# Attention followed by a mixture of experts on one core: expert blocks chosen from step 1 on, two to four steps ahead, with GpSimd padding the last ones

## The chip, the core and the metric

The kernel runs on one core of one Trainium2 chip. The metric is the device time of one execution in microseconds (us); less is better. Beside it stands a profile of one execution: its span is the time from the first to the last instruction.

## What is computed

Four batches of 5056 tokens go through a channel attention (256 x 256 per batch), and each of the 20224 resulting tokens goes through one of eight experts.

```python
# attention, for each batch; q, k, v are (4, 5056, 256)
qn = q / (norm(q, axis=1) + 1e-6);  kn = k / (norm(k, axis=1) + 1e-6)
a = softmax(kn.T @ qn / tau)                      # 256 x 256
x = (v @ a).reshape(20224, 256)

# routing: one expert of eight per token
logits = x @ w_gate + modality_bias[modality_id]
e_idx = argmax(logits, axis=1);  gate_w = softmax(logits)[e_idx]

# experts: w1 is (8, 256, 1024), w2 is (8, 1024, 256)
for e in range(8):
    mask = e_idx == e
    out[mask] = gate_w[mask, None] * (relu(x[mask] @ w1[e]) @ w2[e])
```

With the inputs used, the routing is uneven: 10112 tokens go to expert 7, 8704 to expert 4, 1408 to expert 6 and none to the others.

## The kernel before

**Steps.** The tokens are taken in 40 steps of 512 (ten for each batch; the tenth of a batch has 448). Step g does these things:

- `va_pieces`: it loads a tile of v (two buffers), transposes it (`vtp`), multiplies it by the batch's attention matrix (`xp`, 24 matmuls a step) into token rows `x`, and routes them (`route`): per-expert counts by small matmuls (`rp`), a place `pi` for each token, and four indirect DMAs on GpSimd that scatter the rows to `xs` in HBM, where each expert has a stretch of its own. The running end of each expert's rows is `bases[g]`. The load and the transposes of step g+1 stand in step g.
- `kq_pieces`: for the next batch (so in steps 0 to 29) it loads a tile of q and of k, splits each into a high and a low part, and adds their product to the 256 x 256 matrix `g`. The first batch's q and k work stands before step 0.
- at the first step of a batch, `softmax_pieces` makes the attention matrix.

**Blocks.** The experts work on blocks of 512 rows of one expert (40 blocks; the last two have 384 rows). At the end of a step, `pick` chooses a block on VectorE: among the experts that have at least 512 rows not yet taken, the one with the lowest number. It writes the first row and the expert's number to `pki`. If no expert has 512 rows, it takes spare rows behind all experts, which are filled with zeros and an out-of-range token number. `slots_by(g)` says how many blocks are chosen by step g; `START` sets the first. A chosen block goes to the list `waiting` and is begun `LAG` steps later.

`block_pieces` makes a block's pieces: `load_w` (register loads of `pki` on SyncE, then two halves of `w1` and `w2` into `w1r` and `w2r`, three buffers each), `load_x` (the block's rows from `xs` into `xr`, after all scatters of the steps up to the choice and after the pads), `split_w` (weights into high and low parts, ScalarE and VectorE), `tr_x` (transposes `xtp`), `m1` (`hp`, relu into `hh` and `hl`), `m2` (`y`) and `finish` (scaled rows `yo`, scattered to the output by GpSimd). The weights and rows of a block are loaded at the start of the step before it begins; its `split_w` and `tr_x` are put into the second half of the body of the block before it. For the first block they stand at the end of the step before.

**Order.** `_interleave` merges the pieces of a step's block, its attention work and its q and k work in proportion. The program's scheduler then fixes the order of the instructions of each engine when the program is built; an engine runs them in that order and waits where something is missing. SyncE issues all loads, GpSimd all scatters.

**Buffers in the first steps.** As long as no block runs, q and k of the second batch borrow the blocks' buffers: loads use `w1r` and `w2r` for `2 <= s < START + 2`, splits use `xh` and `xl`, squares `hh` and `hl` for `s < START + 1`. Steps before `first_block = LAG + START` use the blocks' PSUM buffers for transposes and routing.

**The end.** After step 39, SyncE writes a block of pad rows behind the last row of each expert (eight DMAs of 516 KB, each at a row number read by a register load). Then the remaining blocks run; the last three ("tail" blocks, slots 37 to 39) are chosen among all rows that are left, full blocks first. Behind them stands a conditional part for rows still left, which is not entered with these inputs.

Of the kernel before, what the change touches and what calls it, by code (L numbers as in the profile page):

```python
# [34 lines left out]
def kernel(  # L35
# [35 lines left out]
    LAG = 4  # L71
# [10 lines left out]
    const = ctx.enter_context(tc.tile_pool(name="const", bufs=1))  # L82
    p1 = ctx.enter_context(tc.tile_pool(name="p1", bufs=1))
# [45 lines left out]
    eid9 = const.tile([1, E + 1], F32, name="eid9")  # L129
    nc.vector.memset(eid9, 0.0)  # L130
    nc.vector.tensor_copy(eid9[:, 0:E], iof[0:1, :])
    prio9 = const.tile([1, E + 1], F32, name="prio9")
    nc.vector.memset(prio9, 0.5)
    nc.vector.tensor_copy(prio9[:, 0:E], desc[0:1, :])
    inc9 = const.tile([1, E + 1], F32, name="inc9")
    nc.vector.memset(inc9, 0.0)
    nc.vector.memset(inc9[:, 0:E], float(BLK))
    nxt9 = const.tile([1, E + 1], F32, name="nxt9")
    nc.vector.memset(nxt9, float(E * CAP))
    nc.vector.tensor_copy(nxt9[:, 0:E], base0[0:1, :])  # L140
    end9 = const.tile([1, E + 1], F32, name="end9")
    nc.vector.memset(end9, float(E * CAP + BLK))

    xs = dram.tile([ROWS, XW], F32, name="xs")
    pad = {}
# [6 lines left out]
    pads = []  # L152
    written = [[] for _ in range(G)]

    def pad_rows(r):
        ins = nc.sync.dma_start(
            xs[bass.ds(r, BLK), :].rearrange("(p t) c -> p t c", t=BLK // P),
            pad[0].unsqueeze(1).to_broadcast([P, BLK // P, XW]),
        )
        pads.append(ins.ins)  # L160
        tc.declare_no_dep(
            ins.ins, group="xr", reason="pads go past the last row of an expert, and before the blocks with them"
        )

    small = {}
# [274 lines left out]
    first_block = LAG + START  # L440

# [122 lines left out]
    def tiles(slot):  # L564
        return TT - 1 if NB_MIN - SHORT <= slot < NB_MIN else TT

    def pick(g, slot, tail):
        nc.vector.tensor_copy(end9[:, 0:E], bases[g][0:1, :])
        sh = [1, E + 1]
        rem = p2.tile(sh, F32, tag="rem", name=f"rem_{slot}")  # L570
        nc.vector.tensor_tensor(rem, end9, nxt9, ALU.subtract)
        pr = p2.tile([1, 2, E + 1], F32, tag="pr", name=f"pr_{slot}")
        if tail:

            full = pr[:, 1, 0:E]
# [6 lines left out]
        m = p2.tile([1, 1], F32, tag="pm", name=f"pm_{slot}")  # L582
# [4 lines left out]
        pk = p2.tile([1, 2], F32, tag="pk", name=f"pk_{slot}")  # L587
        nc.vector.tensor_reduce(pk, pr, AX.X, ALU.add)
        pki = p4.tile([1, 2], I32, tag="pki", name=f"pki_{slot}")
        nc.vector.tensor_copy(pki, pk)  # L590
        nc.vector.scalar_tensor_tensor(rem, rem, tiles(slot) / TT, inc9, ALU.mult, ALU.mult)
        nc.vector.tensor_tensor(nxt9, nxt9, rem, ALU.add)
        return pki

    FH = FF // 2
    JH = NJ // 2
    FCH = 2 * P

    def block_pieces(g, slot, pki, tail):
        st = {"wr": {}, "wc": {}, "h": {}}  # L600
        tt = tiles(slot)
        rows = tt * P
# [1 line left out]
        def load_x():  # L604
            r = nc.sync.value_load(pki[0:1, 0:1], min_val=0, max_val=E * CAP)
            xr = p3.tile([P, TT, XW], F32R, tag="xr", name=f"xr_{slot}")
            ins = nc.sync.dma_start(
                xr[:, 0:tt, :].bitcast(F32), xs[bass.ds(r, rows), :].rearrange("(p t) c -> p t c", t=tt)
            )
# [140 lines left out]
    for s in range(NS):  # L750
        run(kq_pieces(0, s))
        if s == 0:
            load_small()
            make_pad("pad0")
            pad_rows(E * CAP)
    setup_bias(0)
    run(softmax_pieces(0))
    setup_bias(1)
# [12 lines left out]
    def block_stream(blk, nxt):  # L771

        once(blk, "load")
        once(blk, "prep")
        body = list(blk["body"])
        if nxt is not None:
            once(nxt, "load")
            done.add((nxt["slot"], "prep"))
            at = [len(body) * (i + 4) // 8 for i in range(len(nxt["prep"]))]
            for o, f in reversed(list(zip(at, nxt["prep"]))):  # L780
                body.insert(o, f)
        before = open_blk[0]["last"] if open_blk[0] is not None else []
        open_blk[0] = blk
        return [blk["first"]] + before + body
# [3 lines left out]
    for g in range(G):  # L788
        b, s = divmod(g, NS)
        streams = []  # L790
        for gg, blk in waiting:
            if gg <= g - LAG + 1:
                once(blk, "load")
        if len(waiting) > 0 and waiting[0][0] <= g - LAG:
            _, blk = waiting.pop(0)
            streams.append(block_stream(blk, waiting[0][1] if waiting and waiting[0][0] <= g - LAG + 1 else None))
# [5 lines left out]
        if waiting and waiting[0][0] <= g - LAG + 1:  # L802
# [44 lines left out]
    def left_over(slot, n):  # L847
        if n <= 0:
            return
        rem = p1.tile([1, E + 1], F32, tag="lrem", name=f"lrem_{slot}")  # L850
        nc.vector.tensor_tensor(rem, end9, nxt9, ALU.subtract)
# [44 lines left out]
```

## Time and profile before

| | |
|---|---|
| median of 3 runs | 1243.62 us (1242.7 to 1243.8) |
| the profiled execution | 1244.48 us, span 1242.2 us |
| mean granted TensorE clock | 0.996 |
| TensorE (PE) busy | 1222.2 us, 98% |
| its weight loads (PEld) | 1115.3 us, 90% |
| VectorE (DVE) busy | 843.0 us, 68% |
| ScalarE (ACT) busy | 755.0 us, 61% |
| GpSimd (POOL) busy | 347.9 us, 28% |
| HBM read and written | 167.06 MB and 46.34 MB |

How the rows below are read: the page cuts the span into 40 equal slices and gives for each the busy share in tenths, and the granted clock (PEclk) likewise. A row of a timeline has the start and the duration in us, engine, line, operation and tiles, and in square brackets the idle time before it and what ended it. A row of waits says who waited for whom: us in total, times, longest. A row of DMA issues has the issuing queue, how many, their size, and the median us from issue to landing. SPq is SyncE's queue of DMA issues. `L523` is line 523 of the kernel.

### The profile page before, as it was taken

To read this page: it belongs to the slowest core of one execution; us is meant where nothing else is said; L and a number is where in the kernel's file an instruction comes from. 1 tells how busy PE (TensorE), PEld (TensorE's weight loads), DVE (VectorE), ACT (ScalarE), POOL (GpSimd) and SP (SyncE) were. 2 spreads that over 40 slices of the span, in tenths; PEclk is the share of its full clock that TensorE was granted. 3 is DMA by queue.
4 is the path that set the end of the run, shared out by engine and by line. 5 is a ranking of instruction groups with operands and counts; after the bars stand their busy time and mean duration, and the time that the engine had idled before them with its cause. 6 is when DMAs were issued, how large, how long until landed. Compare 5 with 4: busy or idle time off the path is not lost.

```text
span 1242.2 us, 23800 instructions
## 1 busy us (share of the span) xinstructions
PE 1222.2 (98%) x8316; PEld 1115.3 (90%) x8316; DVE 843.0 (68%) x2215; ACT 755.0 (61%) x1531; POOL 347.9 (28%) x348
## 2 busy tenths in 40 slices
PE   7998999999999999999999999999999999999997
PEld 6897999999999999999999999999999999999997
DVE  7997967767777667867677776666655666665552
ACT  7885856766666666766666665565555555545553
POOL 0135243232222222322222222222432222321121
PEclk9998999999999999999999999999999999999999
DMA  9769864565555555555555554444554443467320
GB/s 321 245 207 302 262 197 155 160 194 176 173 178 173 171 171 171 168 171 170 174 185 183 171 166 136 136 135 147 162 178 153 143 153 121 147 208 222 119 95 29
DMA packets 113026, 215.06 MB, mean 173 GB/s; under 512 B 16128, under 2 KB 61696, under 8 KB 112896
## 3 DMA queue, kind: packets, MB, share of 16 engines
q1 hardware_dynamic: 97632, 171.84, 44.2%
q0 software_dynamic: 15264, 41.60, 8.8%
q8 instruction: 67, 1.10, 0.4%
q14 instruction: 63, 0.52, 0.1%
HBM read 167.06 MB, written 46.34 MB: 172 GB/s over the span
## 4 chain that ended last, share of the span: by engine, by line
PE 89%; issue 3%; DVE 3%; DMA 2%; ACT 1%; POOL 1%; SPq 0%; POOLq 0%; DVEq 0%; ACTq 0%
PE hp L677 34%; PE y L697 34%; PE xp L487 9%; PE g L283 4%; PE vtp L471 2%; PE g L287 2%; PE xtp L659 2%; DMA k<-in_k_dram 1%; POOL out_dram L418 1%; PE selfk L294 0%; DVE acc L274 0%; DMA xs<-x,pi 0%; DVE ks L258 0%; DMA xr<-xs 0%; DMA q<-in_q_dram 0%
## 5 line engine op out<-in xcount | busy, mean ns | idle before, releaser
L697 PE MATMUL y<-w2h,hh 128*128 128x256 f32 x1264 | 356.8, 282 | 0.6 <-ACT yo L713 0.6
L418 POOL DMA_INDIRECT xs<-x,pi x160 | 171.9, 1074 | 660.9 <-ACT w1h L645 480.3
L697 PE MATMUL y<-w2l,hh 128*128 128x256 f32 x1264 | 352.9, 279 | 0.0
L697 PE MATMUL y<-w2h,hl 128*128 128x256 f32 x1264 | 351.8, 278 | 0.1
L683 DVE SCALAR_TENSOR_TENSOR hl<-hp,hh 128x512 fp32r<-128x512 f32 (+1 forms) x320 | 216.5, 677 | 145.8 <-ACT hh L682 145.5
L682 ACT ACTIVATE hh<-hp 128x512 fp32r<-128x512 f32 (+1 forms) x320 | 190.2, 594 | 170.4 <-PE hp L677 168.5
L677 PE MATMUL hp<-xh,w1h 128*128 128x512 f32 (+1 forms) x640 | 256.7, 401 | 0.2 <-ACT xh L664 0.2
L677 PE MATMUL hp<-xl,w1h 128*128 128x512 f32 (+1 forms) x640 | 251.3, 393 | 0.0
L677 PE MATMUL hp<-xh,w1l 128*128 128x512 f32 (+1 forms) x640 | 250.7, 392 | 0.0
L697 PEld LDWEIGHTS y<-w2h,hh 128*128 128x128 f32 x1264 | 237.5, 188 | 12.6 <-ACT yo L713 0.8
L697 PEld LDWEIGHTS y<-w2l,hh 128*128 128x128 f32 x1264 | 238.1, 188 | 10.0
L697 PEld LDWEIGHTS y<-w2h,hl 128*128 128x128 f32 x1264 | 236.7, 187 | 0.4 <-DVE hl L683 0.3
L418 POOL DMA_INDIRECT out_dram<-yo,xr x158 | 162.5, 1029 | 157.5 <-ACT yo L713 113.9
L649 DVE TENSOR_TENSOR w2l<-w2r,w2h 128x512 fp32r<-128x512 f32 x160 | 110.3, 690 | 71.8 <-ACT w2h L645 71.7
L645 ACT CAST w2h<-w2r 128x512 fp32r<-128x512 f32 x160 | 100.0, 625 | 77.4 <-PE y L697 68.4
L649 DVE TENSOR_TENSOR w1l<-w1r,w1h 128x512 fp32r<-128x512 f32 x160 | 109.8, 687 | 52.1 <-ACT w1h L645 51.8
L677 PEld LDWEIGHTS hp<-xh,w1l 128*128 128x128 f32 x640 | 120.7, 189 | 26.3
L645 ACT CAST w1h<-w1r 128x512 fp32r<-128x512 f32 x160 | 100.9, 631 | 55.6 <-PE hp L677 55.2
L677 PEld LDWEIGHTS hp<-xl,w1h 128*128 128x128 f32 x640 | 121.0, 189 | 14.0 <-DVE xl L665 0.2
L677 PEld LDWEIGHTS hp<-xh,w1h 128*128 128x128 f32 x640 | 120.6, 189 | 13.6 <-ACT xh L664 0.3
L283 PE MATMUL g<-qs,ks 128*128 128x512 f32 (+1 forms) x320 | 120.5, 400 | 6.7 <-DVE qs L258 5.5
L487 PE MATMUL xp<-ah,vh 128*128 128x264 f32 x320 | 96.1, 301 | 0.1
(152 smaller groups left out, 1829.6 us busy)
## 6 DMA issues: line engine op xcount, KB each, us to landing
w1r<-in_moe_w_dram SPq DMA_DIRECT2D x80, 512.0 KB, 3.4
w2r<-in_moe_w_dram SPq DMA_DIRECT2D x80, 512.0 KB, 3.7
xr<-xs SPq DMA_DIRECT2D x38, 516.0 KB, 4.8
v<-in_v_dram SPq DMA_DIRECT2D x36, 512.0 KB, 5.3
q<-in_q_dram SPq DMA_DIRECT2D x35, 512.0 KB, 8.1
k<-in_k_dram SPq DMA_DIRECT2D x35, 512.0 KB, 5.7
xs<-pad SPq DMA_DIRECT2D x9, 516.0 KB, 6.0
xs<-x,pi POOLq DMA_INDIRECT x160, 5.0
```

What stands on the lines that cost most here:

```text
L283: nc.tensor.matmul(g, ks[:pp, t, m * P : (m + 1) * P], qs[:pp, t, :], start=first, stop=False, skip_group_check=True,)
L287: nc.tensor.matmul(g[:, 0:C], ks[:pp, t, C + m * P : C + (m + 1) * P], qs[:pp, t, 0:C], start=False, stop=last, skip_group_check=True,)
L418: ins = nc.gpsimd.indirect_dma_start(out=dst, out_offset=bass.IndirectOffsetOnAxis(ap=idx, axis=0), in_=rows, in_offset=None, bounds_check ...
L471: nc.tensor.matmul(tp[:, t * P : (t + 1) * P], st["v"][:, t, h * P : (h + 1) * P], ident, is_transpose=True, start=t == 0, stop=True, skip ...
L487: nc.tensor.matmul(xp[:, 0:DE], a[:, h, t * P : (t + 1) * P], w[:, h, :], start=i == 0, stop=i == len(seq) - 1,)
L645: ins = nc.scalar.copy(hi, src).ins
L649: nc.vector.tensor_tensor(lo, src, hi.bitcast(F32), ALU.subtract)
L659: nc.tensor.matmul(tp[:, t * P : (t + 1) * P], st["xr"][:, t, h * P : (h + 1) * P], identr, is_transpose=True, start=t == 0, stop=True, sk ...
L677: nc.tensor.matmul(hp[:, 0:rows], w[:, h, fs], x[:, h, 0:rows], start=i == 0, stop=i == len(seq) - 1)
L682: nc.scalar.activation(hh[:, 0:rows], hp[:, 0:rows], AF.Relu)
L683: nc.vector.scalar_tensor_tensor(hl[:, 0:rows], hp[:, 0:rows], 0.0, hh[:, 0:rows].bitcast(F32), ALU.max, ALU.subtract)
L697: ins = nc.tensor.matmul(y, a[:, tsl], w[:, j % 2, :], start=(j == 0 and i == 0 and t % 2 == 0), stop=(j == NJ - 1 and i == 2), skip_group ...
```

## The change

The first block is chosen in step 1 instead of 3, and no block is chosen in steps 7 and 13. A block is begun four steps after its choice up to the one chosen in step 6, three steps after for those of steps 8 to 12, and two steps after from step 14 on, so that one block begins in each step from 5 to 39. The pads behind the experts' ends are gone, apart from the spare rows. Instead `pick` runs on 128 partitions, and for a tail block it works out, for each of the block's rows past the expert's last, its place in `xs`; GpSimd scatters pad rows there (four or three indirect DMAs per tail block; rows that hold tokens get a number out of range, and nothing is written for them). The block's `load_x` waits for those scatters.

```diff
-    START = 3
+    START = 1
+
+    SKIP = (7, 13)
...
+    rowid = {TT: eid[:, E + 1 : E + 1 + TT], TT - 1: eid[:, E + 1 + TT : E + 2 * TT]}
+    for tt in rowid:
+        nc.gpsimd.iota(io_i[:, 0:tt], pattern=[[1, tt]], base=0, channel_multiplier=tt)
+        nc.vector.tensor_copy(rowid[tt], io_i[:, 0:tt])
...
     def slots_by(g):
-        return max(0, g + 1 - START)
+        return max(0, g + 1 - START - sum(x <= g for x in SKIP))
+
+    def lag(g):
+        n = LAG
+        for x in SKIP:
+            n -= g >= x + n
+        return n
...
     def pick(g, slot, tail):
...
+        if not tail:
+            return pki, pads
+        tt = tiles(slot)
+        row = room[:, 4 * (E + 1) : 4 * (E + 1) + tt]
+        nc.vector.tensor_scalar(row, rowid[tt], pk[:, 2:3], float(BADTOK), ALU.is_lt, ALU.mult)
+        at = pki[:, 2 : 2 + tt]
+        nc.vector.scalar_tensor_tensor(at, rowid[tt], pk[:, 0:1], row, ALU.add, ALU.add)
+        return pki, [
+            scatter(
+                xs[:, :], at[:, t : t + 1], pad[0], ["x", "xr"] + [f"x{i}" for i in range(G)], [], ROWS - 1,
+                "past the last row of an expert, and before the block with them",
+            )
+            for t in range(tt)
+        ]
...
-            after(ins.ins, pads if tail else pads[:1])
+            after(ins.ins, padded)
...
-            if gg <= g - LAG + 1:
+            if gg <= g + 1 - lag(g + 1):
                 once(blk, "load")
-        if len(waiting) > 0 and waiting[0][0] <= g - LAG:
+        if len(waiting) > 0 and waiting[0][0] <= g - lag(g):
...
-    endi = p1.tile([1, E], I32, tag="endi", name="endi")
-    nc.vector.tensor_copy(endi, bases[G - 1][0:1, :])
+    p1.tile([P, 8], F32, tag="filler", name="filler")
     make_pad("pad1")
-    for e in range(E):
-        r = nc.sync.value_load(endi[0:1, e : e + 1], min_val=0, max_val=E * CAP)
-        pad_rows(r)
```

More of the change, by code (lines that the diff above doesn't have):

```diff
@@ L127 @@
     nc.vector.tensor_scalar(base0, iof, float(CAP), None, ALU.mult)
[L129 to L132, printed above, removed]
+    eid = const.tile([P, 16], F32, name="eid9")
+    nc.vector.memset(eid, 0.0)
+    eid9 = eid[:, 0 : E + 1]
+    nc.vector.tensor_copy(eid9[:, 0:E], iof)
+    prio9 = const.tile([P, E + 1], F32, name="prio9")
     nc.vector.memset(prio9, 0.5)
-    nc.vector.tensor_copy(prio9[:, 0:E], desc[0:1, :])
-    inc9 = const.tile([1, E + 1], F32, name="inc9")
+    nc.vector.tensor_copy(prio9[:, 0:E], desc)
+    inc9 = const.tile([P, E + 1], F32, name="inc9")
     nc.vector.memset(inc9, 0.0)
     nc.vector.memset(inc9[:, 0:E], float(BLK))
-    nxt9 = const.tile([1, E + 1], F32, name="nxt9")
+    nxt9 = const.tile([P, E + 1], F32, name="nxt9")
     nc.vector.memset(nxt9, float(E * CAP))
-    nc.vector.tensor_copy(nxt9[:, 0:E], base0[0:1, :])
-    end9 = const.tile([1, E + 1], F32, name="end9")
+    nc.vector.tensor_copy(nxt9[:, 0:E], base0)
+    end9 = const.tile([P, E + 1], F32, name="end9")
     nc.vector.memset(end9, float(E * CAP + BLK))
+    rowid = {TT: eid[:, E + 1 : E + 1 + TT], TT - 1: eid[:, E + 1 + TT : E + 2 * TT]}
+    for tt in rowid:
+        nc.gpsimd.iota(io_i[:, 0:tt], pattern=[[1, tt]], base=0, channel_multiplier=tt)
+        nc.vector.tensor_copy(rowid[tt], io_i[:, 0:tt])
     xs = dram.tile([ROWS, XW], F32, name="xs")
@@ L153, with pad_rows @@
     written = [[] for _ in range(G)]
-    def pad_rows(r):
+    def pad_rows():
         ins = nc.sync.dma_start(
-            xs[bass.ds(r, BLK), :].rearrange("(p t) c -> p t c", t=BLK // P),
+            xs[E * CAP : E * CAP + BLK, :].rearrange("(p t) c -> p t c", t=BLK // P),
             pad[0].unsqueeze(1).to_broadcast([P, BLK // P, XW]),
@@ L161, in pad_rows @@
         tc.declare_no_dep(
-            ins.ins, group="xr", reason="pads go past the last row of an expert, and before the blocks with them"
+            ins.ins, group="xr", reason="no expert has rows there"
         )
@@ L567, in pick @@
     def pick(g, slot, tail):
-        nc.vector.tensor_copy(end9[:, 0:E], bases[g][0:1, :])
-        sh = [1, E + 1]
-        rem = p2.tile(sh, F32, tag="rem", name=f"rem_{slot}")
+        nc.vector.tensor_copy(end9[:, 0:E], bases[g])
+        n = 3 if tail else 2
+        room = p2.tile([P, 4 * (E + 1) + TT], F32, tag="pr", name=f"pr_{slot}")
+        pr = room[:, 0 : 3 * (E + 1)].rearrange("p (a e) -> p a e", a=3)
+        rem = room[:, 3 * (E + 1) : 4 * (E + 1)]
         nc.vector.tensor_tensor(rem, end9, nxt9, ALU.subtract)
-        pr = p2.tile([1, 2, E + 1], F32, tag="pr", name=f"pr_{slot}")
         if tail:
+            nc.vector.tensor_copy(pr[:, 2, :], rem)
             full = pr[:, 1, 0:E]
@@ L586, in pick @@
         nc.vector.tensor_tensor(pr[:, 1, :], rem, eid9, ALU.mult)
[L587 to L590, printed above, removed]
+        if tail:
+            nc.vector.tensor_tensor(pr[:, 2, :], rem, pr[:, 2, :], ALU.mult)
+        pk = p2.tile([P, 3], F32, tag="pk", name=f"pk_{slot}")
+        nc.vector.tensor_reduce(pk[:, 0:n], pr[:, 0:n, :], AX.X, ALU.add)
+        pki = p4.tile([P, 2 + TT], I32, tag="pki", name=f"pki_{slot}")
+        nc.vector.tensor_copy(pki[0:1, 0:2], pk[0:1, 0:2])
         nc.vector.scalar_tensor_tensor(rem, rem, tiles(slot) / TT, inc9, ALU.mult, ALU.mult)
         nc.vector.tensor_tensor(nxt9, nxt9, rem, ALU.add)
-        return pki
+        if not tail:
[12 more added lines that the diff above has]
+        ]
     FH = FF // 2
@@ L597, with block_pieces @@
     FCH = 2 * P
-    def block_pieces(g, slot, pki, tail):
+    def block_pieces(g, slot, picked, tail):
+        pki, padded = picked
         st = {"wr": {}, "wc": {}, "h": {}}
@@ L754 @@
             make_pad("pad0")
-            pad_rows(E * CAP)
+            pad_rows()
     setup_bias(0)
@@ L791 @@
         for gg, blk in waiting:
-            if gg <= g - LAG + 1:
+            if gg <= g + 1 - lag(g + 1):
                 once(blk, "load")
-        if len(waiting) > 0 and waiting[0][0] <= g - LAG:
+        if len(waiting) > 0 and waiting[0][0] <= g - lag(g):
             _, blk = waiting.pop(0)
-            streams.append(block_stream(blk, waiting[0][1] if waiting and waiting[0][0] <= g - LAG + 1 else None))
+            streams.append(block_stream(blk, waiting[0][1] if waiting and waiting[0][0] <= g + 1 - lag(g + 1) else None))
         soft = list(softmax_pieces(b)) if s == 0 and b > 0 else []
@@ L801 @@
         _interleave(*streams)
-        if waiting and waiting[0][0] <= g - LAG + 1:
+        if waiting and waiting[0][0] <= g + 1 - lag(g + 1):
             once(waiting[0][1], "load")
@@ L850, in left_over @@
         rem = p1.tile([1, E + 1], F32, tag="lrem", name=f"lrem_{slot}")
-        nc.vector.tensor_tensor(rem, end9, nxt9, ALU.subtract)
+        nc.vector.tensor_tensor(rem, end9[0:1, :], nxt9[0:1, :], ALU.subtract)
         left = p1.tile([1, 1], F32, tag="left", name=f"left_{slot}")
```

2 lines of the change are left out of this document (1 added, 1 removed).

## The prediction

> **What bounds the kernel now.** I read the page's shares and slices first, then the chain, then stretches of time cut where the slices change, then the waits around the one hole.
>
> ```profile
> span 1242.2 us, 23800 instructions
> PE 1222.2 (98%) x8316; PEld 1115.3 (90%) x8316; DVE 843.0 (68%) x2215; ACT 755.0 (61%) x1531; POOL 347.9 (28%) x348
> PE   7998999999999999999999999999999999999997
> PEclk9998999999999999999999999999999999999999
> PE 89%; issue 3%; DVE 3%; DMA 2%; ACT 1%; POOL 1%; SPq 0%; POOLq 0%; DVEq 0%; ACTq 0%
> ...
> 50.00:93.62 43.62, 43.18 (x317) 39.23 (x316) 41.34 (x137) 37.91 (x88) 12.61 (x12) 1.00 0.64 220
> 93.62:108.20 14.58, 14.49 (x104) 12.54 (x102) 13.68 (x65) 10.80 (x26) 10.03 (x12) 1.00 0.87 275
> 108.20:112.27 4.07, 0.08 (x1) 0.02 (x1) 1.87 (x8) 2.03 (x5) 3.15 (x4) 0.96 0.92 243
> 112.27:119.10 6.83, 6.66 (x24) 4.83 (x25) 3.42 (x15) 1.74 (x4) 0.41 (x1) 0.53 1.06 392
> 119.10:1209.00 1089.90, 1089.64 (x7442) 996.27 (x7441) 731.65 (x1887) 655.98 (x1326) 307.91 (x296) 1.00 0.52 167
> ...
> PE xtp L659 <- DMA xr<-xs: 4.0, 1, 4.0
> ```
>
> In the stretches, the first number is the length, then PE, PEld, DVE, ACT and POOL busy, the granted clock, the DMA share and GB/s. TensorE does nothing else from 119.1 to 1209: 1089.64 of 1089.90 us. There is nothing to win there, only to lose. The one hole that this change can reach is at 108.2: TensorE idles for 4.07 us, 4.0 of them for the first block's rows (`xr<-xs`), and then runs 6.83 us at a granted clock of 0.53. The second costs 6.83 x (1 - 0.53) = 3.2 us. So 7.2 us is the most that a perfect start of the blocks could bring.
>
> **The change, part by part.**
>
> *Work.* Before, blocks are chosen at the ends of steps 3 to 39 (37) and begun four steps later; seven are left after step 39. After, they are chosen in steps 1 to 39 without 7 and 13 (also 37) and begun in steps 5 to 39, so five are left. Blocks stay 40 and matmuls the same. Two blocks move from behind step 39 into steps 5 and 6. TensorE is full on both sides of that move, so the move itself is worth nothing; what counts is when the first block can start.
>
> *The first block.* It now needs the rows of steps 0 and 1 instead of 0 to 3, and its transposes `xtp` stand in the program behind step 4 instead of step 6.
>
> ```profile
> 78.78 0.19 PE L523 MATMUL rp<-oh,trim 128*128 128x32 bf16 x1
> 88.50 0.97 POOL L418 DMA_INDIRECT xs<-x,pi  x1 [0.30 <-issue]
> 90.61 0.19 PE L523 MATMUL rp<-oh,trim 128*128 128x32 bf16 x1
> 93.50 0.28 PE L287 MATMUL g<-qs,ks 128*128 128x256 f32 x1
> 93.63 0.60 PE L471 MATMUL vtp<-ident,v 128*128 128x128 f32 x4
> 95.77 0.15 DVE L590 CAST pki<-pk 1x2 int32<-1x2 f32 x1
> 97.02 0.41 SPq L626 DMA_DIRECT2D w1r<-in_moe_w_dram  x1
> 99.58 1.17 POOL L418 DMA_INDIRECT xs<-x,pi  x1 [0.30 <-issue]
> 106.89 0.35 SPq L607 DMA_DIRECT2D xr<-xs  x1
> 108.00 0.28 PE L287 MATMUL g<-qs,ks 128*128 128x256 f32 x1
> 112.28 1.24 PE L659 MATMUL xtp<-identr,xr 128*128 128x128 f32 x8 [4.00 <-DMA xr<-xs]
> L487 PE MATMUL xp<-ah,vh 128*128 128x264 f32 x40 | 11.8, 300 | 0.0
> xs<-x,pi POOLq DMA_INDIRECT x10, 3.5
> xs<-x,pi POOLq DMA_INDIRECT x17, 5.5
> w1r<-in_moe_w_dram SPq DMA_DIRECT2D x5, 512.0 KB, 8.1
> xr<-xs SPq DMA_DIRECT2D x38, 516.0 KB, 4.8
> ```
>
> When does TensorE get there? A step has 8 such `xp` matmuls (4 tiles, 2 halves), so the 40 that the groups of 50 to 93.62 show are steps 0 to 4. At 93.63 come the transposes of v for row group 6, which belong to step 5. So step 4's matmuls end at 93.6 and step 6's at 108.3; the 14.65 us between are steps 5 and 6.
>
> When do the rows get there? Steps leave four scatters each on POOL, and the sixteenth, the last of step 3, starts at 99.58; `xr` is issued 7.31 us later, and the transposes start at 112.28, 12.70 us after that scatter. The eighth, the last of step 1, starts at 88.50. TensorE finished step 1's routing matmul at 78.78 already, but POOL works off its scatters one by one, (99.58 - 88.50) / 8 = 1.39 us each or 5.5 us a step, and is the slower of the two. So the block's rows come 11.08 us earlier (99.58 - 88.50), while TensorE comes 14.65 us earlier. With the same 12.70 us behind the last scatter, `xtp` starts at 88.50 + 12.70 = 101.20, the idle time grows from 4.00 to 7.57 us, and the end moves by 14.65 - 11.08 = **+3.57 us**. The clock price of 3.2 us stays.
>
> The 12.70 us is one end. In the calm stretch of 76 to 92 the scatters landed in 3.5 us, between 93 and 125 in 5.5, because the block's weights were loaded at the same time (8.1 us each). With 3.5, 0.1 for the issue and the page's 4.8 for `xr`, the transposes start at 96.9 and the end moves by -0.7 us. I take +3.57: the choice `pki` comes 5.2 us after its step's routing matmul (90.61 to 95.77), so the weights (1.25 us behind it at 97.02) fall on the last scatters in the new place as in the old. [...]
>
> *Smaller buffers for steps 2 to 4* (q and k no longer borrow `w1r`, `w2r`, `xh`, `xl`, `hh`, `hl` there): they can delay TensorE before 93.6. Nothing is charged, since it would then wait less for rows that POOL and DMA set; with TensorE on time again the price is the 7.57 us of cover.
>
> *Distance 4 to 3 to 2.* From step 16 on a block is chosen in step g, loaded in g+1 and begun in g+2. SP then waits for `pki` before the weights and for that step's scatters before `xr`; q, k and v loads queue behind it. The tightest steps are those without q and k work:
>
> ```profile
> 972.14 0.19 PE L523 MATMUL rp<-oh,trim 128*128 128x32 bf16 x1
> 976.23 0.16 DVE L590 CAST pki<-pk 1x2 int32<-1x2 f32 x1 [0.19 <-DVE rem L591]
> 978.73 0.97 POOL L418 DMA_INDIRECT xs<-x,pi  x1 [0.31 <-issue]
> SPq L454 <- PE vtp L471: 75.3, 31, 7.2
> 991.38 0.45 PE L659 MATMUL xtp<-identr,xr 128*128 128x128 f32 x4
> xs<-x,pi POOLq DMA_INDIRECT x95, 5.5
> 1079.32 0.19 PE L523 MATMUL rp<-oh,trim 112*128 112x32 bf16 x1
> 1085.82 0.94 POOL L418 DMA_INDIRECT xs<-x,pi  x1 [0.30 <-issue]
> 1142.29 0.46 PE L659 MATMUL xtp<-identr,xr 128*128 128x128 f32 x4
> 1165.34 0.46 PE L659 MATMUL xtp<-identr,xr 128*128 128x128 f32 x4
> ```
>
> From the last scatter to the next step's `xtp` there are 991.38 - 978.73 = 12.65 us. Scatter 5.5 (median over 300 to 1000), issue 0.1, load 4.8: 10.4 us, so 2.3 us are left. With the long chain above, 12.70, it is late by 0.05 us. The loads behind SP's wait are of no weight: v has two buffers, its load goes out when transposes free one (the row of SP's waits), and the next step's v lies in the other; q and k have two as well. I charge 0; the range keeps up to 1 us in each of the ten last steps. Once more, at the loop's end, where a block takes 1165.34 - 1142.29 = 23.05 us: the last chosen block would have `xtp` at 1142.29, and step 39's last scatter would stand two blocks later than now, 1085.82 + 46.1 = 1131.9; 10.4 us against 10.4. I charge 0, at most 2.3.
>
> *Pads.* Eight 516 KB writes leave SP, and ten indirect scatters join POOL, at 0.97 to 1.17 us each, four before a tail block's `xr`. The first tail block's `xtp` at 1165.34 stands 39.9 us behind the routing matmul at 1079.32 + 46.1; step 39's last scatter starts 6.5 us behind that matmul, four outputs and four pads follow (8 x 1.27 us: 0.97 and the 0.30 before it), landing and load take 10.4: 27 us. Cover 13 us; cost nothing. Choosing on 128 partitions instead of one costs nothing: the `pki` cast takes 0.16 us, and VectorE is busy 68%. The new iotas at the start lie beside the first loads.
>
> **Sum.** 0 + 3.57 + 0 + 0. The profiled execution took 1244.48 us around its span of 1242.2, 0.86 above the median of 1243.62. So 1248.0 by that run, **1247.2** by the median; the forecast's own range is 1243 to 1250.
>
> **Rivals.**
>
> *A, faster: TensorE does not stop behind step 4.* The order of each engine's instructions is fixed when the program is built. If it puts work of step 5 ahead of `xtp`, the 7.57 us until 101.2 are filled: 7.57 of the 14.65 us fit in. Then the wait (4.0) and the half clock (3.2) vanish: 1243.6 - 7.2 = 1236.4; with up to 3 us left idle, 1239.4; I take 1238. For it: step 5's work is ready at 93.6, as before shows by doing it. Against it: at 108.2 the same order left TensorE idle, with step 7's transposes of v not put ahead. [...]
>
> *B, short chain:* -0.7 us, idle 3.3 us: 1242.9 with the half clock, 1239.7 without.
>
> *C, much slower: rows late in every step.* The four weight loads, now spread over a step, all go out behind `pki` at 976.2 and meet the scatters up to 979. Each us beyond 12.65 costs TensorE a us, in 10 to 24 steps; with 1 us in ten, 1247.2 + 10 = 1257. Against it are the 2.3 us by the medians.
>
> *D: a choice finds no full expert* and takes the spare rows: a block is wasted. Counted from the reference's inputs, expert 7 has exactly 512 rows after step 1, and at most 504 and 500 are there in steps 7 and 13, so every choice finds one; a wrong row would cost a block of 23 us and more, over 1266.
>
> **How the numbers follow.** Forecast 0.42, A 0.33, B 0.08, C 0.12, D 0.02, something not seen 0.03. 0.2% is 2.5 us, about what this kernel's measurement can tell. Slower: 0.30 of the forecast, C, D: 0.44. Faster: 0.30 of A, 0.04 of B, 0.01 of the forecast: 0.35. The rest, 0.21, same. The range goes from A's end, 1236.4, to C's 1257; outside remain D and half of a heavier C.
>
> **What would show it.** Right: one wait of `xtp` on `xr<-xs` of 6 to 8 us starting near 94, a clock near 0.5 behind it, and no PE idle from there to the tail. Wrong: an idle time under 3 us and a full clock in the fourth slice (A); many waits of `xtp` on `xr<-xs` after step 16 (C); 48 more `hp` matmuls (D).

## The result, and the profile after

| | median | range, runs |
|---|---|---|
| before | 1243.62 us | 1242.7 to 1244.47, 5 |
| after | 1251.4 us | 1249.37 to 1253.11, 5 |

The ratio is 1.0059, 95% interval 1.0046 to 1.0072: the change costs 7.8 us. The profiled execution of after took 1249.37 us around a span of 1247.6 us and is the fastest of its runs, so its rows show some 2 us less of the loss than the median; that of before took 0.9 us more than its median. The two profiled executions are 4.9 us apart, their spans 5.4 us. One of the six runs of e11_fill1, further below, took 1704.82 us at a granted clock of 0.65 where the others had 0.99 and more, and its time below is the median of the other five.

The page of after, the same lines as those shown of before:

```profile
span 1247.6 us, 23733 instructions
PE 1225.5 (98%) x8316; PEld 1115.6 (89%) x8316; DVE 849.6 (68%) x2228; ACT 756.8 (61%) x1531; POOL 360.9 (29%) x360
PE   8998999999999999999999999999999999999997
PEclk9999999999999999999999999999999999999999
PE 19%; DMA 3%; issue 2%; DVE 2%; ACT 1%; POOL 1%; SPq 0%; POOLq 0%; ACTq 0%
```

The matmuls are the same 8316. No slice shows the loss, since a slice is 31 us long and the waits are short. What is new stands in the chain: its shares add up to 28%, so it could be followed back for only some 350 us, into the last batch (before: nearly the whole span, 89% of it on PE). Three of its five longest links are weight loads:

```profile
969.56 4.83 DMA w1r<-in_moe_w_dram
997.77 4.89 DMA w1r<-in_moe_w_dram
1135.69 4.97 DMA w1r<-in_moe_w_dram
```

The stretches. The hole is cut at the same events as in the prediction, and the stretch behind it takes in the low clock; 860, 1160 and 1211 are fixed times. The columns are as in the prediction; the number behind the x is how many instructions started there.

```profile
50.00:93.90 43.90, 43.28 (x310) 38.57 (x309) 41.40 (x164) 35.11 (x81) 14.25 (x14) 1.00 0.64 206
93.90:97.50 3.60, 0.30 (x3) 0.06 (x1) 1.01 (x5) 1.45 (x4) 2.69 (x4) 1.00 0.94 269
97.50:104.00 6.50, 6.16 (x28) 4.77 (x29) 4.17 (x14) 2.83 (x7) 1.29 (x2) 0.74 1.04 381
104.00:860.00 756.00, 755.66 (x5157) 689.46 (x5155) 539.15 (x1366) 482.40 (x977) 220.80 (x209) 1.00 0.52 172
860.00:1160.00 300.00, 295.06 (x2007) 267.12 (x2007) 183.15 (x532) 158.21 (x322) 88.97 (x88) 1.00 0.46 151
1160.00:1211.00 51.00, 51.00 (x344) 47.15 (x343) 26.30 (x41) 27.18 (x53) 17.38 (x17) 1.00 0.40 134
```

The stretch of 860 to 1160 of the kernel before, for comparison:

```profile
860.00:1160.00 300.00, 300.00 (x2053) 274.94 (x2052) 180.43 (x493) 159.62 (x322) 86.37 (x84) 1.00 0.51 163
```

Two things are to be seen. The hole at the first block got no worse: 3.60 us instead of 4.07, and the clock behind it is 0.74 over 6.5 us instead of 0.53 over 6.83, which costs 6.5 x 0.26 = 1.7 us instead of 3.2. And TensorE, which had no gap between 860 and 1160, now has one: 46 matmuls fewer start in the same 300 us. At 300 / 2053 = 0.146 us each that is 6.7 us. Most of the 300 us belong to the last batch's steps, which have no q and k work; the 756 us before them lose nothing.

A count between fixed times depends on what falls into them (e5_pads below has 2047 without any idle time). Cut at events it is more: from the end of the last `g` to the end of the last `y` the kernel before takes 1234.58 - 805.97 = 428.6 us, and the changed one 1241.52 - 850.15 = 391.4 us with two blocks fewer in it. At the prediction's 23.05 us a block that is 8.9 us lost, 4.8 of them as idle time of TensorE. Ahead of the last `g`, 1.9 us are won (44.2 us later, with 46.1 us more work before it), and behind the last `y` 1.5 us: together the 5.4 us between the spans.

The waits of after between 860 and 1160 (who waited for whom, us in total, times, longest); none of these rows appears in that stretch of before:

```profile
ACT w1h L680 <- DMA w1r<-in_moe_w_dram: 18.5, 10, 2.4
PEld y L732 <- DVE hl L718: 4.6, 9, 0.9
PE y L732 <- DVE hl L718: 2.7, 7, 0.7
PEld y L732 <- ACT hh L717: 2.4, 5, 0.8
PE xtp L694 <- DMA xr<-xs: 1.6, 1, 1.6
```

Ten times ScalarE's cast of `w1` stands still for a weight load, 1.85 us on average, and twice that of `w2` (2.8 us in all). TensorE itself hardly waits for a transfer (1.6 us, once); it waits for relu. One of the ten, from the timeline of after:

```profile
996.66 0.16 DVE L611 CAST pki<-pk 1x2 int32<-1x2 f32 x1 [0.18 <-DVE pr L612]
997.77 0.38 SPq L661 DMA_DIRECT2D w1r<-in_moe_w_dram  x1
999.90 0.39 PE L712 MATMUL hp<-xh,w1l 128*128 128x512 f32 x1
1002.74 0.62 ACT L680 CAST w1h<-w1r 128x512 fp32r<-128x512 f32 x1 [2.37 <-DMA w1r<-in_moe_w_dram]
1003.26 0.59 ACT L717 ACTIVATE hh<-hp 128x512 fp32r<-128x512 f32 x1
1003.91 0.38 PE L732 MATMUL y<-w2h,hh 128*128 128x256 f32 x1 [0.40 <-ACT hh L717]
1004.00 0.69 DVE L718 SCALAR_TENSOR_TENSOR hl<-hp,hh 128x512 fp32r<-128x512 f32 x1
1004.74 0.39 PE L732 MATMUL y<-w2h,hl 128*128 128x256 f32 x1 [0.33 <-DVE hl L718]
```

Read it from the top. The choice is there at 996.82, and 0.95 us later SyncE sends the weights of the block that begins in the next step. ScalarE is done with what stood before at 1000.37, and its next instruction is their cast (`w1h`, line 680), which belongs to the coming block. It waits until 1002.74. The running block's `hp` was finished at 1000.29, so its relu (`hh`, line 717) could have run at 1000.37. It stands behind the cast and runs at 1003.26, almost 3 us late. TensorE uses up what it has and stops twice, at 1003.51 for `hh` and 0.9 us later for `hl`. In before, at distance 4, none of ScalarE's casts between 860 and 1160 waits for a weight load.

### The profile page after: what moved, and what is told of

It is laid out like the page before. It is cut to its first block, busy times and chain, and to the rows that moved or that the text cites. A ratio compares the mean times of both kernels' runs of the same rounds, so it can differ in the third digit from the quotient of the medians.

```text
span 1247.6 us, 23733 instructions
## 1 busy us (share of the span) xinstructions
PE 1225.5 (98%) x8316; PEld 1115.6 (89%) x8316; DVE 849.6 (68%) x2228; ACT 756.8 (61%) x1531; POOL 360.9 (29%) x360
```

## The experiments

The theories after the result: **W**, the weights come late at distance 2 and hold up ScalarE's cast, relu and TensorE; **P**, the pads and the choice on 128 partitions cost; **R**, the rows `xr` come late in every step. Each run's ratio is to runs of the kernel before on the same chip.

**e1_dist4: the distance stays 4.**

```diff
-            n -= g >= x + n
+            n -= 0
```

> The change with one part undone: choices stay in steps 1 to 39 without 7 and 13, but every block is begun four steps after its choice, so steps 11 and 17 begin none and seven blocks are left after step 39. Theory W (short distance makes the weights late): at distance 2 the loads of w1 and w2 go out only behind the choice, all four at once; ScalarE's cast of w1 stands ahead of a relu in its queue, waits up to 2.4 us for the load, and TensorE waits for the relu, about 1 us in each of the ten steps of the last batch. With distance 4 this goes: about 8 to 9 us less than the changed kernel, 1241 to 1243 us, ScalarE's waits for w1r near 0 after 860 us. Theory P (the loss is in the pads or in choosing on 128 partitions): no change, 1250 to 1252 us. Theory R (rows xr late): also faster, but then the changed kernel's waits of TensorE for xr should have carried it, and they sum to 1.6 us after 860.

Measured: 1244.33 us, ratio 0.9999 (0.9988 to 1.0010). Of the 7.8 us, 7.1 are gone. The last batch is whole again (2052 matmuls against 2053 in before; from the last `g` to the last `y` 428.7 us against 428.6, with 2925 matmuls in both):

```profile
860.00:1160.00 300.00, 300.00 (x2052) 274.94 (x2051) 182.89 (x505) 160.66 (x324) 93.77 (x93) 1.00 0.45 147
```

The time is 1.3 us above what W expected. The early start is still in this kernel and brings nothing; more on that with e3_start2.

**e4_castlater: distances as in the change, only the cast moved.** The first high-part cast of a block stands behind the running block's latest relu in ScalarE's order.

```diff
+    relu = [None]
...
                 ins = nc.scalar.copy(hi, src).ins
+                if 0 < slot < NB_MIN and ci == 0 and n == "w1":
+                    order(ins, [relu[0]])
...
-            nc.scalar.activation(hh[:, 0:rows], hp[:, 0:rows], AF.Relu)
+            relu[0] = nc.scalar.activation(hh[:, 0:rows], hp[:, 0:rows], AF.Relu).ins
```

> The changed kernel with distances as they are (4, 3, 2); only the first cast of each next block's w1 is tied behind the last relu written before it in the program, which puts it two relus later in ScalarE's order. The loads are as late as before, but nothing of the running block stands behind them. Theory W: TensorE's waits for hl and hh in the last batch go, 1242 to 1245 us. Theory R (rows late) or P (pads): no change, 1249 to 1252 us. If the late weights cost by crowding the DMA engines rather than through ScalarE's queue, also no change.

Measured: 1245.06 us, ratio 1.0005 (0.9993 to 1.0017). The weights go out as late as in the change, and 6.3 of the 7.8 us are gone. What is left of the loss in the last batch, from its window, then its wait for rows:

```profile
860.00:1160.00 300.00, 296.80 (x2043) 271.86 (x2042) 185.61 (x535) 162.64 (x329) 89.14 (x89) 1.00 0.47 154
```

```profile
PE xtp L697 <- DMA xr<-xs: 3.1, 3, 1.6
```

Ten matmuls fewer than before (1.5 us), and no wait of the `w1` cast for weights any more. From the last `g` to the last `y` it takes 386.1 us, where the change takes 391.4 for the same 2621 matmuls. The 3.1 us on `xr` are theory R, in three steps of the ten. So W is confirmed by two different edits, R is a small part, and P is not needed.

**e6_dist42: the distance without the early start.** START goes back to 3; distances 4, 3, 2 stay. As two steps still choose nothing, five blocks instead of three are chosen behind step 39, with 18 pad scatters instead of 10.

```diff
-    START = 1
+    START = 3
```

> START=3 with SKIP=(7,13): the first block is chosen in step 3 and begun in step 7 as in the kernel before, and the distance falls to 3 and 2 as in the changed kernel, so two blocks more stay behind the loop. Theory W (weights that come late at distance 2 hold up ScalarE's cast and with it relu and TensorE): the last batch between 860 and 1160 loses 7 to 9 us, none of it in steps 16 to 29, total 1250 to 1253 us. Theory S (the late loss needs the early start, since five instead of seven blocks behind the loop leave the last batch short of work): no loss behind 860, 1243 to 1245 us.

Measured: 1253.79 us, ratio 1.0077 (1.0063 to 1.0092), 9.9 us above before, more than the 7 to 9 expected. The window and the waits of the last batch:

```profile
860.00:1160.00 300.00, 294.28 (x1986) 267.05 (x1985) 180.92 (x529) 155.00 (x311) 95.78 (x94) 0.99 0.45 146
```

```profile
ACT w1h L680 <- DMA w1r<-in_moe_w_dram: 15.1, 9, 2.3
PEld y L732 <- DVE hl L718: 6.9, 7, 2.8
PE y L732 <- DVE hl L718: 5.4, 7, 2.6
DVE pki L611 <- DMA xs<-pad,pki: 2.9, 1, 2.9
```

67 matmuls fewer, 9.8 us; from the last `g` to the last `y` 439.8 us, 11.2 more than before for the same 2925 matmuls. Nearly the whole difference of the two spans (11.9 us) lies here, and theory S falls. Not all of it is the weights, though. The longest wait, 2.6 us from 1111.94 on, comes from the pads: VectorE's cast of the last choice (`pki`) waits for a pad scatter until 1113.27, and the `hl` that TensorE needs stands behind it. The clock then falls to 0.50 for 3.41 us (0.99 over the window above, 1.00 in before), another 1.7 us. Without these 4.3 us some 7 remain, as W expected. The profiled execution is the slowest of the six (1256.19 us); no trace shows whether the others have this wait too. The run is 2 us slower than the change itself, but the two intervals of the ratio overlap.

**e5_pads: the pads and the choice alone** (START 3, no step left out, distance 4).

```diff
-    START = 1
-    SKIP = (7, 13)
+    START = 3
+    SKIP = ()
```

> START=3, SKIP=(): the first block is chosen in step 3 and begun in step 7 at distance 4, as in the kernel before; what stays of the change is the pads (no pad writes at experts' ends, padding scatters of GpSimd for the tail blocks), the choice on 128 partitions and the smaller set-up. Theory W (the loss sits in the short distance alone): these parts cost nothing, 1243.0 to 1244.8 us, an idle time of about 4 us ahead of the first xtp near 108 as before, no stalls behind 860. Theory P (pads and the choice carry a part): 1246 to 1250 us, with idle time of PE at the first tail blocks (behind 1145) or waits of VectorE on pr, pk or pki.

Measured: 1242.5 us, ratio 0.9990 (0.9980 to 0.9999). The pads and the choice cost nothing; if anything they give 1 us. P falls as the cause of the loss, though with the 18 pad scatters of e6_dist42 a choice did hold up TensorE once.

**e2_gap30: the distance goes back up to 3 by leaving step 30 without a block.**

```diff
-        return n
+        return n + (g >= 30)
```

> The change with the distance one step longer from step 30 on: step 30 begins no block, and the blocks behind it are begun three steps after their choice; six are left after step 39. Steps 16 to 29 keep distance 2. Theory W with the loss only in the last batch, where a step is 27 us long and not 30: the loss of 8 us after 860 goes, 1241.5 to 1244 us, while ScalarE's waits for w1r between 400 and 860 (28 us in the changed kernel) stay and cost TensorE nothing. If distance 2 also costs in steps 16 to 29: 1246 or more. Theory P: 1250 to 1252 us.

Measured: 1255.21 us, ratio 1.0091 (1.0074 to 1.0109): a miss by 11 us. The window of step 30 and the rest, and the waits between 850 and 880:

```profile
837.00:899.00 62.00, 54.88 (x350) 48.99 (x349) 34.09 (x115) 29.61 (x62) 11.58 (x12) 0.89 0.42 140
899.00:1178.00 279.00, 279.00 (x1908) 255.69 (x1907) 169.85 (x475) 148.56 (x300) 90.98 (x90) 1.00 0.46 148
```

```profile
PE atp L384 <- DVE ssm L375: 3.6, 1, 3.6
PE rp L539 <- DVE sm L559: 1.9, 1, 1.9
```

From 899 on nothing is lost, as W says. But step 30 makes the last batch's attention matrix, and its chain of small operations has no block's matmuls beside it now: 62.00 - 54.88 = 7.1 us idle, and 0.11 x 62 = 6.8 us of clock at most. I had taken a step without a block for free. The two that e1_dist4 has (11 and 17) are, but those have q and k work and no softmax.

**e3_start2: start one step later than the change, one step left out, distance 4 to 3.**

```diff
-    START = 1
-    SKIP = (7, 13)
+    START = 2
+    SKIP = (13,)
```

> First choice in step 2, none in step 13 alone, so the first block is begun in step 6 and the distance falls from 4 to 3 only. Theory W: at distance 3 the choice lies before the time at which the weights' buffers come free, so nothing is late in the last batch. The first block's wait for its rows lies between that of the changed kernel (3.5 us) and that of the kernel before (4.0 us), with 1.5 to 3.2 us lost to the lower clock. Together 1240 to 1243.5 us: not slower than the kernel before, perhaps the best of all. Theory P: 1247 us or more, as the pads are those of the change.

Measured: 1242.34 us, ratio 0.9987 (0.9976 to 0.9998), the lowest of all kernels here, though level with e5_pads. Distance 3 loses nothing in the last batch. The stretches around its first block:

```profile
94.00:101.90 7.90, 6.68 (x50) 5.96 (x48) 7.64 (x27) 6.58 (x16) 6.71 (x7) 1.00 0.95 310
101.90:104.60 2.70, 0.24 (x2) 0.00 (x0) 1.56 (x11) 1.16 (x4) 1.97 (x3) 1.00 0.90 266
104.60:112.00 7.40, 7.01 (x44) 5.54 (x45) 5.80 (x22) 3.50 (x7) 2.00 (x3) 1.00 1.02 340
```

TensorE waits 2.50 us in the stretch of 2.70, and the clock stays at 1.00 behind it. In this execution that saves the 3.2 us that before pays there, but 1.2 us go at a `rp` ahead of the hole. The mean clock of this execution is 0.999 and that of the eleven other runs 0.995 to 0.997, about that of before, so they will mostly have lost clock after all. The gain is at the edge of what can be measured. An early start is worth little wherever it is put: 1242.5 from step 7 (e5_pads), 1242.34 from step 6, 1244.33 from step 5 (e1_dist4).

**e8_rowsfirst: how long the weights hold up the rows.** From e4_castlater; the first block's rows are loaded ahead of its weights.

```diff
         prep = [lambda: load_w(0), lambda: load_w(1), load_x]
+        if slot == 0:
+            prep = [load_x, lambda: load_w(0), lambda: load_w(1)]
```

> The run e4_castlater with one more edit: the first block's rows are loaded ahead of its four weight loads instead of behind them, so no weights move while step 1's last scatters land. This measures the term of the sum that I took too long (12.70 us from the last scatter's start to xtp, of which 5.5 us for a scatter beside weights, against 3.5 us in a calm stretch). Theory T (weights lengthen the landing): xr goes out 4.0 to 4.8 us behind the start of step 1's last scatter instead of 5.8, and xtp starts about 1.5 us sooner. Theory N: xr goes out 5.5 to 6 us behind it as with the weights ahead. In both, w1h then waits for weights that go out only behind the rows, near 92, and land 7 us or more later, so TensorE stands still for weights near 99 and the time is not below that of e4_castlater: 1245 to 1249 us.

Measured: 1249.98 us, ratio 1.0051 (1.0038 to 1.0065), 1 us above the expected range. The eighth scatter (the last of step 1), the load behind it, and the waits from 85 to 130:

```profile
87.58 0.98 POOL L427 DMA_INDIRECT xs<-x,pi  x1 [0.30 <-issue]
90.34 0.35 SPq L643 DMA_DIRECT2D xr<-xs  x1
```

```profile
ACT w1h L681 <- DMA w1r<-in_moe_w_dram: 5.1, 1, 5.1
PE xp L503 <- ACT x L507: 4.1, 1, 4.1
```

With no weights in flight `xr` goes out 2.76 us behind the scatter's start, against 5.83 in e4_castlater and 5.72 in the change: theory T, and by more than I expected. The time is lost at the same place as in the last batch: the cast waits 5.1 us for weights, and the copy of `x` behind it in ScalarE's order keeps TensorE waiting 4.1 us, now at `xp`, ahead of the block.

**e7_halfw: a half of it, on e3_start2.** The rows go between the two halves of the first block's weights.

```diff
+        if slot == 0:
+            prep = [lambda: load_w(0), load_x, lambda: load_w(1)]
```

> START=2, SKIP=(13,) as in the run e3_start2, and the first block's rows are loaded between the two halves of its weights instead of behind both. Theory T (transfers of weights that go out beside the scatters and the rows lengthen their landing): xr lands about 1 us sooner, the idle time ahead of xtp falls from 2.7 to 1 to 2 us, 1240.5 to 1242 us. Theory N (the scatters' own chain sets the time, the weights are no matter): idle time 2.5 to 3 us as in e3_start2, 1241.8 to 1243 us. If the second half of the weights comes late, hp waits for w1h or w1l near 112 and the time is above 1243.

Measured: 1246.19 us, ratio 1.0018 (1.0009 to 1.0026): the third case of the expectation, earlier than I had put it. The wait for rows falls from 2.5 to 1.6 us as T says, but ScalarE waits 5.1 us for the second half, and TensorE stands still for 2.3 us within the transposes and for 2.4 us ahead of the first `hp`.

**e9_fill2, e10_fill2more, e11_fill1: rival A made true.** Work of the step is put ahead of the first block's transposes, on e3_start2 (40 and 64 empty entries) and on e4_castlater (64).

```diff
+        late = []
+        if blk["slot"] == 0:
+            late = [lambda: None] * 40 + list(blk["prep"])
+            done.add((0, "prep"))
         once(blk, "prep")
...
-        return [blk["first"]] + before + body
+        return late + [blk["first"]] + before + body
...
-            once(waiting[0][1], "prep")
+            if waiting[0][1]["slot"] > 0:
+                once(waiting[0][1], "prep")
```

> The run e3_start2 (first block begun in step 6) with the first block's transposes placed later in TensorE's order: 40 empty entries stand ahead of block 0's pieces when step 6's work is interleaved, so that step's 8 transposes of v and 12 xp matmuls (8 x 0.11 + 12 x 0.12 = 2.3 us) come ahead of xtp. Theory F (rival A of the prediction: work of the step that stands ahead of xtp fills the wait for the rows): the idle time ahead of xtp falls from 2.67 us to 0.4 to 1.0 us, 1239.5 to 1241.5 us. Theory G (nothing won: the work moved ahead was not lost, and what it displaced waits elsewhere, for vh, attention or the block's casts): 1242 to 1244 us with new idle time between 105 and 130.

> As e9_fill2 with 64 empty entries instead of 40: one more tile's xp matmuls (18, and 8 transposes: 3.1 us) stand ahead of xtp, more than the 2.67 us of idle time. Theory F: no idle time over 0.5 us ahead of xtp, 1239 to 1241.2 us. Theory G: 1242 to 1245 us, since the block's relu and casts crowd into the rest of the step and TensorE waits there.

> The run e4_castlater (first block begun in step 5, distances 4 to 2, cast placed later) with the same 64 empty entries: 8 transposes and 18 xp matmuls, 3.1 us, stand ahead of xtp, whose wait was 3.3 to 3.5 us. Theory F: the idle time falls to 0.2 to 0.8 us and the granted clock stays at 1.00 from 94 to 112 (it was 0.75 and 0.68 in two stretches of 6 us), together 5 to 6 us less: 1239 to 1241 us. If the clock falls for another reason than the idle time (the DMA load, the transposes), only the idle part comes back: 1241.5 to 1243 us. Theory G: 1244 to 1246 us.

Measured: 1247.42 (ratio 1.0032, 1.0021 to 1.0043), 1246.65 (1.0023, 1.0013 to 1.0034) and 1248.55 us (1.0049, 1.0033 to 1.0066). The wait for the rows is gone in all three, and all three are slower than the kernels they come from. The waits of e10_fill2more from 85 to 135 and the two stretches at the new hole:

```profile
PE g L292 <- ACT ks L266: 4.7, 1, 4.7
ACT qs L266 <- DMA q<-in_q_dram: 4.7, 1, 4.7
```

```profile
115.80:120.60 4.80, 0.19 (x2) 0.00 (x0) 2.00 (x4) 2.54 (x6) 0.00 (x0) 0.81 1.04 374
120.60:127.00 6.40, 6.34 (x25) 5.69 (x26) 4.29 (x7) 3.36 (x9) 0.00 (x0) 0.61 0.62 249
```

The hole stands some 14 us later than in e3_start2 and is longer (4.7 us of waiting instead of 2.5): TensorE waits for q's cast, and that for a load of q that went out behind 2 MB of weights of the second block, with the 16 DMA engines fully taken (1.04). The part of theory F that says that the wait can be filled holds; the part that says it is then won does not.

**e12_nextlater: the second block's loads behind q and k**, on e10_fill2more.

```diff
-            if gg <= g + 1 - lag(g + 1):
+            if gg <= g + 1 - lag(g + 1) and not (blk["slot"] == 1 and g == first_block):
                 once(blk, "load")
...
-            once(nxt, "load")
+            if nxt["slot"] > 1:
+                once(nxt, "load")
...
+            if nxt["slot"] == 1:
+                body.insert(1, lambda: once(nxt, "load"))
```

> The run e10_fill2more with one more edit: in the first block's step the loads of the second block's weights and rows are issued behind that step's loads of q and k instead of ahead of them (SP's order: xr of block 0, q, k, then four weight loads). In e10_fill2more the wait for the rows was gone, but g then waited 4.8 us for ScalarE's cast of q, whose load stood behind 2 MB of weights that are needed only a step later, and the granted clock fell to 0.57 and 0.87 in the next two stretches of 6 us. Theory D (the hole was handed on through SP's order and the DMA engines; with q and k ahead it is closed): no idle time over 1.5 us between 95 and 130, clock 1.00 from 106 to 130, 4.7 + about 3.4 us less than e10_fill2more: 1238 to 1240.5 us, the fastest of all. Theory E (the DMA engines are full at 1.0 in these stretches whatever the order, so the second block's weights come late in its place): idle time of 3 us and more near 120 to 130, 1243 to 1247 us.

Measured: 1245.9 us, ratio 1.0011 (1.0002 to 1.0020). Neither theory, though the time lies in E's range: the second block's weights come in time, but `g` now stands directly behind `xp`, at 105.7, and waits 3.9 us for q and k. Their loads went out at 100.81 and 101.37, right behind `xr`, for which SyncE's queue had waited 7.9 us until the scatters had landed. Whether a full reordering of the loads between 90 and 125 would close the hole stays open; between 106 and 118 the DMA engines are at 1.03 to 1.04 in this run too.

## Why the prediction came out as it did

The forecast was 1247.2 us and slower; it is 1251.4 and slower. The way was right by luck: the term that gave it, +3.57 us at the first block, came out at -0.2 us, and the loss came from a term that I had charged at 0.

**The first block, +3.57 us: sized wrong.** In after:

```profile
86.74 0.97 POOL L427 DMA_INDIRECT xs<-x,pi  x1 [0.30 <-issue]
92.46 0.35 SPq L642 DMA_DIRECT2D xr<-xs  x1
97.47 0.77 PE L694 MATMUL xtp<-identr,xr 128*128 128x128 f32 x7 [3.30 <-DMA xr<-xs]
```

I had 88.50 for the scatter and 12.70 us behind it, together 101.20. The scatter started 1.76 us earlier, and the chain took 97.47 - 86.74 = 10.73 us. TensorE came as expected (last `g` at 93.89), so the idle stretch was 3.60 us (3.30 of them the wait) and not 7.57. The end moves by 14.65 - (112.28 - 97.47) = -0.2 us, and the clock gives back 3.2 - 1.7 = 1.5 us. That is rival B in size, though its short chain of 8.4 us was not reached: the weights do lengthen it, by 5.72 - 2.76 = 3.0 us (e8_rowsfirst). My error was to carry over the 12.70 us from a place where the four weight loads start 2.6 us ahead of the last scatter (97.02 against 99.58). In the new place the first starts 4.6 us ahead (82.13 in after), so less of them is still moving then; that this makes the 2 us is argued, not measured.

**The clock price "stays": wrong.** In the profiled execution of after the clock was 0.50 for 3.41 us behind the hole, in that of before for 6.83 us. That is one execution each: the mean clock was 0.998 in this one and 0.996 to 0.997 in the four others of after, so they may have paid more. Instead of the expected 6 to 8 us of `xtp` on `xr` near 94 there were 3.30, and TensorE stopped in the last batch, where I had expected no idle time.

**Distance 4 to 3 to 2, charged 0: the step that failed.** I worked out only the rows, by 12.65 us against 10.4. For them the answer was nearly right: R costs 1.6 us in after and 3.1 in e4_castlater, within the "up to 1 us in each of the ten last steps". For the weights I went by SyncE's queue and by who stands behind it on SyncE and said nothing of who stands behind their reader on ScalarE. The price was 7.1 us by e1_dist4 and 9.9 by e6_dist42, whose profile has 4.3 us of another cause in it. The prediction had both ends of it in hand: weights go out 1.25 us behind `pki`, and took 8.1 us (median of 93 to 125) to land. In after they land in 5.7 (median) where they took 3.4 before, from the pages of the two kernels, after first:

```profile
w1r<-in_moe_w_dram SPq DMA_DIRECT2D x80, 512.0 KB, 5.7
```

```profile
w1r<-in_moe_w_dram SPq DMA_DIRECT2D x80, 512.0 KB, 3.4
```

Rival C saw the four loads in a burst and its size (10 us) but had the burst delay the rows and TensorE directly; the delay went through ScalarE.

A late instruction of ScalarE held up the one behind it: `hp` was done at 1000.29, and its relu ran at 1003.26, directly behind the cast, which had waited 2.37 us for its weights. With the first cast of each block placed behind a relu, 6.3 of the 7.8 us are gone (e4_castlater).

**Pads and the choice, 0:** right (e5_pads: 1.35 us less than before on the same chip, hardly measurable). **Smaller buffers, 0:** TensorE is idle 0.62 of the 43.90 us before 93.90, against 0.44 of 43.62 before, so right within 0.2 us. **The loop's end, 0:** the last chosen block's `xtp`, at 1149.19, does not wait for its rows, and none of the 51 us from 1160 to 1211 is idle, so right; in e4_castlater, where TensorE gets there earlier, it waits 1.6 us (at 1144.84), within the 2.3. **Work, 0:** right, 8316 matmuls in both.

**Rival A:** the order did leave TensorE idle, as forecast. Making it true (e9, e10 and e11) won nothing. That up to 3 us could be left idle at the full clock was my estimate, and no run shows such a border: the clock stayed at 1.00 behind 2.50 us (e3_start2) and was 0.52 over the 6.80 us behind 2.93 us (e1_dist4). **Rival C's** sign, many waits of `xtp` on `xr` after step 16, did not appear: two, together 1.9 us, behind 400.

**The sum as measured:** by the times, the pads and the choice -1.1, the start and the steps left out 1244.33 - 1242.5 = +1.8, the distance 1251.4 - 1244.33 = +7.1, together +7.8. These runs come from different chips, on which before had medians of 1243.62 to 1243.93; by the ratios, each to before on its own chip, the three are -1.2, +1.1 and +7.5. The first two are as large as their uncertainty: by e6_dist42 and the change the start gives 2.4 us instead of costing 1.8, and the profile of after has it at -0.2 - 1.5 = -1.7.

## What to carry to other kernels

When a load is brought closer to its use, ask of its first reader not only whether it is late but what stands behind it in its engine's order: a cast that prefetches for the next block can stop the relu that this block needs. Place such instructions behind the work of the present block (e4_castlater: 6.3 of 7.8 us back with the load as late as ever). And before filling a hole, look at what the loads behind it are waiting for: here, with the DMA engines full behind the first block (a share of 1.04 in e10_fill2more), moving matmuls into the hole moved it by 14 us.

## What the chip showed that I had not expected

- The price of an idle time does not follow its length in this kernel. TensorE waited 2.50 us for `xr` in e3_start2, and the clock stayed at 1.00; 2.93 us in e1_dist4 (3.30 - 0.37, the stretch and TensorE's busy time in it), and the clock was 0.50 for 6.83 us; 3.30 us in after, 0.50 for 3.41 us; 4.00 us in before, 0.50 for 6.83 us. (The 2.70, 3.60 and 4.07 above are stretches that include the end of the matmul before the wait.) In e11_fill1 4.14 us (6.00 - 1.86, from 106 to 112) were followed by only 3.41 us. The stretch of e1_dist4, with a little of the full clock behind it:

```profile
100.20:107.00 6.80, 6.63 (x23) 5.24 (x23) 4.17 (x14) 2.38 (x6) 1.62 (x2) 0.52 1.03 357
```

Between 50 and 1209 us the granted clock is either 1.00 or 0.50 in the traces of before and after, and the one time at 0.50 lasts 6.83 us in before and 3.41 us in after. The mean clocks of other runs' windows fit times at 0.50 of 3.41 us (0.72 over 6 us in e11_fill1), 6.83 us (0.75 and 0.68 over 6 us each in e4_castlater) and 10.24 us (0.88, 0.50 and 0.76 over 6 us each in e7_halfw; in e2_gap30 10.24 and 3.41 us together, 0.89 over 62 us): once, twice and three times 3.41. At half the clock that is a price of at most 1.7, 3.4 or 5.1 us, an estimate from these lengths.

No run here settles why 2.93 us were followed by twice the time at 0.50 that 3.30 us were, and 2.50 us by none.

- A scatter of 128 rows landed soon enough for the next load to go out 2.76 us behind its start when no weights were moving (e8_rowsfirst), and 5.72 us when four loads of 512 KB were (after).
- In after, ScalarE's cast waited for weights in steps 16 to 29 as well (14 times, 28.2 us between 400 and 860), and TensorE lost nothing there (755.66 of 756 us busy). I take it that the q and k matmuls of those steps gave it other work; no run took them away to show it. The same wait cost TensorE time only in the last batch, which has no such work.
